# An attention block with a gated bilinear FFN: PSUM redistributed between score slots and free banks, x transposed on TensorE, a halved Q buffer and a longer ring

## The chip, the core and the metric

The kernel runs on one core of a Trainium2 chip. The metric is device microseconds for one execution. The core has five engines that matter here: PE (TensorE, matmuls), ACT (ScalarE, here the exponential), DVE (VectorE), POOL (GpSimd) and SP, which issues most DMAs. PE writes its results to PSUM, which this kernel divides into eight banks of 128 x 512 float32 values. Executions of one kernel spread here (the changed kernel: 801.4 to 813.0 us in four), so times below come with their runs, and the main argument rests on profiles, in which the same time can be followed item by item.

Ratios are computed as the mean time of one kernel's fast runs over the mean of the other's fast runs of the same rounds, so they are not quite the ratios of the medians quoted beside them.

## The reference, cut to what matters

```python
# x: [1, 2048, 512] bf16; 32 heads of 16; F = 1376
g = sigmoid((x * gate_w).sum(-1, keepdims=True))
q, k, v = split(x @ wqkv)                      # 32 heads
p = softmax(q @ k.T * 16 ** -0.5)              # 32 x 2048 x 2048 scores
a = (p @ v) @ wo
b = ((x @ w_gate) * (x @ w_up)) @ w_down
return g * a + (1 - g) * b
```

The 32 x 2048 x 2048 scores set the time. They are cut into 2048 **units** of 128 keys x 512 queries, one PSUM bank each. Four units (four heads of one parity) on the same 128 keys form an **entry**, and 16 entries form a **group**; there are 32 groups.

## The kernel before

An order model inside the kernel builds one static program for each engine. Each unit takes one of two routes. ACT reads two or three banks of scores at once and writes exp to a ring PT in SBUF. Or DVE clamps the scores to int16 (one bank at a time, buffer I2), then makes four integer copies of the whole entry (LL and I2 again), which read as bf16 approximate exp. PE then multiplies by V ("PV"), accumulating in psO. All other matmuls (K, Q, V, FFN, output projection) are **fill units**: they need a bank for a few matmuls and one eviction by DVE.

The eight banks are two score slots of three, one for PV and one free bank:

```python
psS = psum_tensor("psS", [128, 3072], F32)   # two slots of three banks
psO = psum_tensor("psO", [128, 512], F32)
psX = psum_tensor("psX", [128, 512], F32)    # the one free bank
```

The third bank of a slot is lent out. When a span of scores is planned, it has three units, or two if the third bank goes to a late fill unit or to a DVE score:

```python
tf, of = third_free(sl)
n, fu, dj = 3, None, None
if tf > max(now, r) + 0.02:
    n = 2
else:
    f = pick_fill(now + 0.3) if now < D_START or F_LATE else None
    if f is not None and f.due + F_LATE <= st["prog"] / 4 and un[0][0][0] < NG - 1:
        n, fu = 2, f                      # a late fill unit takes the third bank
    elif un[0][0][0] == NG - 1 and sl == 0:
        n = 2
    elif not (x_free() and ...) and backlog(now) < D_BACK:
        dj = d_can(now, {j for _, j in un[:2]}, False)
        if dj is not None:
            n = 2                         # a DVE score takes the third bank
```

x comes in transposed by 16 transposing DMAs; Q has two buffers and is asked for 14 entries before its block:

```python
QX = sb("QX", [128, 2, 2, NB, 512], BF16)    # chunk parity, head parity, block
PT = sb("PT", [128, RU, 512], BF16)          # RU = 18
...
o = ld("sp", xT[:, kt, ch * 512 : (ch + 1) * 512],
       x2[ch * 512 : (ch + 1) * 512, kt * 128 : (kt + 1) * 128], ..., transpose=True)
...
n0 = 128 * c + 32 * b - 14                   # Q for row chunk c, block b
fl.append((n0, mk_q(b, c, n0)))
```

In the last group the softmax denominators use one more bank (the third of the first slot), and the tail computes 1/denominator as exp(-ln) in four column slices, Ln then Exp for each slice.

The softmax here doesn't subtract the row's maximum and nothing guards it: scores larger than these inputs give would overflow.

## Time and profile before

857.75 us median of 3 runs (854.71 to 858.06). The profiled execution's span is 858.1 us. It was a further execution of 859.96 us, in the slow state (a lower granted clock, 0.928); it is some 2 us slower than the median, so about 2 us of the account below may be its state.

From the page of the kernel before: busy time by engine, then, in 40 slices of the span, the busy tenths of ACT and DVE and the granted TensorE clock in tenths.

```profile
PE 774.0 (90%) x6164; PEld 200.7 (23%) x6164; DVE 628.9 (73%) x1010; ACT 778.7 (91%) x759; POOL 36.1 (4%) x34
DVE  1326689988989973787998479897967599896401
ACT  1427999999999998899999989999999999999997
PEclk9857969999999999889999999999999999999856
```

ACT is 91% busy and is full from slice 5 on; the first four slices are thin, and there the granted clock falls to 0.5. (The trace's first clock event is at 28.0 us. Up to there the view shows full clock, but the matmuls stand 0.43 us apart, the pace of half clock, so the first digits are not a measurement.) The groups view names what ACT and DVE do. Columns: line, engine, operation, output and input, count, busy us, mean ns of one, idle time just before, and what ended that idle time.

```profile
L1259 ACT ACTIVATE PT<-psS 128x1024 bf16<-128x1024 f32 (+1 forms) x740 | 764.6, 1236 | 71.1 <-PE psS L748 51.7 <-PE psO L987 9.7 <-PE psS L864 7.6
L887 DVE TENSOR_SCALAR I<-psS 128x512 int16<-128x512 f32 x329 | 220.9, 685 | 35.7 <-PE psS L864 34.6
L887 DVE TENSOR_SCALAR I<-psX 128x512 int16<-128x512 f32 x55 | 37.7, 686 | 9.9 <-PE psX L864 9.5 <-PE psS L748 0.2
L918 DVE TENSOR_SCALAR LL<-I 128x2048 int16<-128x2048 int16 x288 | 194.6, 704 | 3.5 <-PE psO L987 2.0
L918 DVE TENSOR_SCALAR I<-I 128x2048 int16<-128x2048 int16 x96 | 70.1, 730 | 1.6
```

L1259 is the exponential: 740 spans, 764.6 us busy, 71.1 us idle before it. L887 is the DVE clamp: 329 scores taken from slot banks (psS) and 55 from the free bank (psX), 384 units in all, so ACT has 2048 - 384 = 1664. L918 makes the copies.

The timeline of ACT from 20 to 70 us (start, duration, operation, count, and in brackets the idle time before and its releaser):

```profile
20.21 4.35 ACT L1259 ACTIVATE PT<-psS 128x1536 bf16<-128x1536 f32 x3 [14.58 <-PE psS L748]
25.04 1.45 ACT L1259 ACTIVATE PT<-psS 128x1536 bf16<-128x1536 f32 x1 [0.48 <-PE psS L748]
30.42 5.48 ACT L1259 ACTIVATE PT<-psS 128x1536 bf16<-128x1536 f32 x4 [3.92 <-PE psS L748]
46.50 5.57 ACT L1259 ACTIVATE PT<-psS 128x1536 bf16<-128x1536 f32 x4 [10.61 <-PE psS L748]
64.28 5.58 ACT L1259 ACTIVATE PT<-psS 128x1536 bf16<-128x1536 f32 x4 [12.20 <-PE psS L748]
```

Between 20 and 70 us ACT sits idle for most of the time, waiting for score matmuls. Stretches of the span (columns: stretch, its length, then busy us and instruction count of PE, PEld, DVE, ACT and POOL, granted clock, DMA share, GB/s):

```profile
40.00:60.00 20.00, 15.04 (x52) 3.21 (x48) 5.61 (x9) 5.57 (x4) 0.00 (x0) 0.50 0.00 1
200.00:300.00 100.00, 96.41 (x834) 25.40 (x832) 92.30 (x150) 100.00 (x103) 2.61 (x2) 1.00 0.07 16
300.00:400.00 100.00, 92.46 (x727) 23.59 (x723) 72.37 (x116) 91.85 (x93) 2.77 (x2) 0.95 0.07 19
```

At 40 to 60 us ACT works 5.6 of 20 us at half the matmul clock. At 200 to 300 us ACT is full and DVE at 92%. At 300 to 400 us ACT loses 8 us and DVE 28.

The span splits along ACT: 20.2 us until the first exponential, 764.6 us of exponentials, 56.5 us of waits between them (71.1 less the 14.6 before the first), and 16.7 us from the last exponential to the end.

### The profile page before, as it was taken

The numbers are of one execution on the slowest core, as the hardware profiler recorded it, in microseconds if no ns is written. First come the engines' busy times: TensorE is split into PE (matmuls) and PEld (weight loads), VectorE is DVE, ScalarE is ACT, GpSimd is POOL, SyncE is SP. The second block draws the span as 40 slices with busy tenths as digits, with TensorE's granted clock in tenths as the row PEclk, the third lists the DMA queues.
The fourth block names the chain that finished last, engine by engine and source line by source line (L and its number), as shares of the span: only waits on it lengthen the run. The fifth ranks groups of instructions, "written<-read, shape, count | busy, mean of one in ns | idle before, by whom it ended". The sixth has DMA issues, their size and how long they took to land.

```text
span 858.1 us, 15166 instructions
## 1 busy us (share of the span) xinstructions
PE 774.0 (90%) x6164; PEld 200.7 (23%) x6164; DVE 628.9 (73%) x1010; ACT 778.7 (91%) x759; POOL 36.1 (4%) x34
## 2 busy tenths in 40 slices
PE   3777998899999999898999999998999999999895
PEld 0111312222222222222222222222222222222211
DVE  1326689988989973787998479897967599896401
ACT  1427999999999998899999989999999999999997
POOL 6000000000000000000000000000000000000000
PEclk9857969999999999889999999999999999999856
DMA  8700000000000000000000010000001100000000
GB/s 153 246 1 1 14 21 13 21 15 20 7 15 21 14 26 20 26 12 10 21 11 21 21 33 12 23 13 9 21 7 28 32 20 15 18 15 8 17 18 24
DMA packets 35657, 22.36 MB, mean 26 GB/s; under 512 B 23012, under 2 KB 30532, under 8 KB 35588
## 3 DMA queue, kind: packets, MB, share of 16 engines
q1 hardware_dynamic: 32420, 19.83, 8.8%
q10 hardware_dynamic: 3168, 1.57, 0.9%
q8 instruction: 48, 0.79, 0.4%
q14 instruction: 21, 0.17, 0.1%
HBM read 10.65 MB, written 2.35 MB: 15 GB/s over the span
## 4 chain that ended last, share of the span: by engine, by line
PE 38%; ACT 32%; DVE 16%; issue 7%; SPq 4%; DMA 3%; ACTq 0%; DVEq 0%
ACT PT L1259 30%; PE psS L748 12%; PE psO L987 10%; DVE I L887 5%; DVE LL L918 5%; PE psX L504 3%; PE psX L426 3%; SPq L410 2%; PE psX L555 2%; DVE I L918 2%; PE psS L555 2%; SPq L1037 1%; DVE VV L434 1%; DMA xT<-in_A_x_dram 1%; PE psX L342 1%
## 5 line engine op out<-in xcount | busy, mean ns | idle before, releaser
L1259 ACT ACTIVATE PT<-psS 128x1024 bf16<-128x1024 f32 (+1 forms) x740 | 764.6, 1236 | 71.1 <-PE psS L748 51.7
L748 PE MATMUL psS<-QX,KT 32*128 32x512 bf16 x1664 | 300.5, 406 | 38.1 <-ACT PT L1259 27.6
L887 DVE TENSOR_SCALAR I<-psS 128x512 int16<-128x512 f32 x329 | 220.9, 685 | 35.7 <-PE psS L864 34.6
L918 DVE TENSOR_SCALAR LL<-I 128x2048 int16<-128x2048 int16 x288 | 194.6, 704 | 3.5 <-PE psO L987 2.0
L987 PE MATMUL psO<-PT,VV 128*32 128x512 bf16 x1664 | 163.9, 407 | 6.9 <-DVE VV L434 6.4
L748 PEld LDWEIGHTS psS<-QX,KT 32*128 32x128 bf16 x1664 | 71.1, 91 | 324.3 <-ACT PT L1259 257.2
L864 PE MATMUL psS<-QX,KT 32*128 32x512 bf16 x329 | 129.0, 392 | 0.2
L987 PE MATMUL psO<-LL,VD 128*32 128x512 bf16 x768 | 72.8, 397 | 0.5 <-DVE LL L918 0.4
L918 DVE TENSOR_SCALAR I<-I 128x2048 int16<-128x2048 int16 x96 | 70.1, 730 | 1.6
L987 PEld LDWEIGHTS psO<-PT,VV 128*32 128x32 bf16 x1664 | 40.0, 96 | 79.5 <-issue 58.5
L1090 POOL TENSOR_TENSOR OT<-onum,rb 128x512 bf16<-128x512 f32 x16 | 22.6, 1415 | 788.8 <-DMA rb<-rscr 788.8
L504 PE MATMUL psX<-xT,wg 128*128 128x512 bf16 (+1 forms) x160 | 51.9, 400 | 1.1 <-DVE usb L518 0.9
L504 PE MATMUL psX<-xT,wu 128*128 128x512 bf16 (+1 forms) x148 | 50.0, 403 | 0.9 <-DVE hT L528 0.5
L887 DVE TENSOR_SCALAR I<-psX 128x512 int16<-128x512 f32 x55 | 37.7, 686 | 9.9 <-PE psX L864 9.5
L987 PE MATMUL psO<-LL,VV 128*32 128x512 bf16 x384 | 39.5, 402 | 4.7 <-DVE LL L918 2.6
L987 PE MATMUL psO<-I,VD 128*32 128x512 bf16 x384 | 39.0, 397 | 2.3 <-DVE I L918 2.2
L434 DVE CAST VV<-psX 128x512 bf16<-128x512 f32 x16 | 11.1, 693 | 31.6 <-PE psX L426 31.6
L426 PE MATMUL psX<-wv,xT 128*128 128x512 bf16 x64 | 28.1, 568 | 5.5 <-DVE VD L447 3.1
L528 DVE TENSOR_TENSOR hT<-psX,usb 128x512 bf16<-128x512 f32 (+1 forms) x40 | 27.3, 682 | 5.5 <-PE psX L504 5.5
L864 PEld LDWEIGHTS psS<-QX,KT 32*128 32x128 bf16 x329 | 30.0, 91 | 1.7 <-DMA QX<-Qst 0.8
L555 PE MATMUL psX<-wd,hT 128*128 128x512 bf16 (+1 forms) x99 | 29.4, 384 | 0.4 <-DVE bsb L566 0.2
L518 DVE CAST usb<-psX 128x512 bf16<-128x512 f32 (+1 forms) x37 | 25.2, 680 | 5.3 <-PE psX L504 5.3
(84 smaller groups left out, 360.9 us busy)
## 6 DMA issues: line engine op xcount, KB each, us to landing
rb<-rscr SPq DMA_DIRECT2D x16, 256.0 KB
onum<-oraw SPq DMA_DIRECT2D x124, 32.0 KB, 2.0
out_dram<-ost SPq DMA_DIRECT2D x16, 128.0 KB, 1.7
QX<-Qst SPq DMA_DIRECT2D x120, 16.0 KB, 1.8
wu<-in_B_w_up_dram SPq DMA_DIRECT2D x1, 1376.0 KB, 6.2
wg<-in_B_w_gate_dram SPq DMA_DIRECT2D x1, 1376.0 KB, 9.0
wd<-in_B_w_down_dram SPq DMA_DIRECT2D x1, 1280.0 KB, 12.2
wv<-in_A_wqkv_dram ACTq DMA_DIRECT2D x1, 512.0 KB, 6.3
```

The costliest lines, as they stand in the source:

```text
L426: return pe.matmul(bk, xT[:, kt, t * 128 : (t + 1) * 128], wv[:, kt, :], start=s0, stop=s1)
L504: return pe.matmul(bk[0:w, :], ws[:, kt, f * 128 : f * 128 + w], xT[:, kt, c * 512 : (c + 1) * 512], start=s0, stop=s1,)
L518: "dve", lambda v: v.tensor_copy(usb[0:w, n % 2, :], un.bank[0:w, :]), deps, **EV
L528: lambda v: v.tensor_tensor(hT[0:w, f, :], un.bank[0:w, :], usb[0:w, n % 2, :], ALU.mult),
L555: return pe.matmul(bk, hT[0:w, f, tt * 128 : (tt + 1) * 128], wd[0:w, f, :], start=s0, stop=s1)
L748: q = pe.matmul(bank_ap(sl, k_), KT[32 * j : 32 * j + 32, b, kt * 128 : (kt + 1) * 128], QX[32 * j : 32 * j + 32, c % 2, p, b, :], start=True,
L864: lambda pe: pe.matmul(bank, KT[32 * j : 32 * j + 32, b, kt * 128 : (kt + 1) * 128], QX[32 * j : 32 * j + 32, c % 2, p, b, :], start=True, ...
L887: lambda v: v.tensor_scalar(I2[:, nb, j, :], bank, _LO, _HI, ALU.max, ALU.min),
L918: lambda v: v.tensor_scalar(dstt, src, 0.5, _BASE + _OFF[k], ALU.mult, ALU.add),
L987: r = pe.matmul((psD if dn else psO)[32 * j : 32 * j + 32, :], ones[:, k_, :] if dn else vcol(m, kt, k_, j), lview(e, k, j) if isd else PT ...
L1090: lambda g: g.tensor_tensor(OT[:, c % 2, b, :], onum[:], rb[:], ALU.mult),
L1259: lambda a: a.activation(PT[:, cells[0] : cells[0] + n, :].rearrange("p a b -> p (a b)"), bank_ap(sl, 0, n), ACT.Exp, scale=_LN2 / _OCT,),
```

## The change

The intent is to give ACT fixed slots of three and two banks, and use the eighth bank as a second free bank that fill units and DVE scores share, so that a DVE score no longer shrinks a span. x is loaded plainly and transposed on PE, to start earlier. Q's buffer is halved, which pays for a ring of 24, and Q is asked for 24 entries ahead. DVE scores are also allowed in the last group. Not shown below: the K units of the start are due three entries earlier than before and the V units one. The core of the diff, with cuts:

```diff
-    RU = 18
+    RU = 24
-    D_LEFT = 6
+    D_LEFT = 4
+    D_LAST = 11
-    FFN_FROM, FFN_TO = 75.0, 490.0
+    FFN_FROM, FFN_TO = 60.0, 490.0
...
-        QX = sb("QX", [128, 2, 2, NB, 512], BF16)
+        QX = sb("QX", [128, 2, NB, 512], BF16)
...
+        xn = SC[:, 0:8192].bitcast(BF16).rearrange("p (t n) -> p t n", t=T)
...
-        psS = ... [128, 3072] ...
+        psS = ... [128, 2560] ...
-        psX = ... [128, 512] ...
+        psX = ... [128, 1024] ...
+        CAP = [3, 2]
+        XB = [psX[:, 0:512], psX[:, 512:1024]]
...
-        for ch in range(NCH):                 # 16 transposing DMAs
-            for kt in range(KD):
-                o = ld("sp", xT[...], x2[...], ..., transpose=True)
+        for t in range(T):                    # 16 plain loads
+            d_xn.append(ld("sp", xn[:, t, :], x2[t * 128 : (t + 1) * 128, :], ...))
...
+        def mk_x(t, due, eng="dve"):          # a fill unit: 4 transposes, 1 copy
+                return pe.transpose(o[:, kt * 128 : (kt + 1) * 128], xn[...], ident[:])
...
-            un = act_units(3)
+            un = act_units(CAP[sl])
...                                            # the choice of n, fu, dj is gone
-                n0 = 128 * c + 32 * b - 14
+                n0 = 128 * c + 32 * b - 24
...
+            xi = x_get(t)                      # a free bank, if there is one
+            if xi is not None:
+                f = pick_fill(t + 0.3)
+                if t > D_START and any(isinstance(x["u"], Unit) for x in xs):
+                    f = None                   # one fill unit at a time after the start
+                if f is not None:
+                    start_fill(f, XB[xi], xs[xi]["op"])
...
+                if s_ready > t + D_GAP:
+                    j = d_can(t, set())
+                    if j is not None:
+                        do_d(j, xi)            # a DVE score in a free bank
```

More of the change, by code (lines that the diff above doesn't have):

```diff
@@ L167, in _build @@
     NE = NG * T
-    RU = 18
+    RU = 24
     D_START = 60.0
-    D_LEFT = 6
+    D_LEFT = 4
+    D_LAST = 11
     D_GAP = 0.3
-    D_BACK = 1.3
-    F_LATE = 6
-    FFN_FROM, FFN_TO = 75.0, 490.0
+    FFN_FROM, FFN_TO = 60.0, 490.0
     VS = H * 17 + 16
@@ L203, in _build @@
         PT = sb("PT", [128, RU, 512], BF16)
-        I2 = sb("I2", [128, 2, 4, 512], I16)
-        LL = sb("LL", [128, 3, 4, 512], I16)
+        SC = sb("SC", [128, 10240], I16)
+        LL = SC[:, 0:6144].rearrange("p (k j n) -> p k j n", k=3, j=4)
+        I2 = SC[:, 6144:10240].rearrange("p (k j n) -> p k j n", k=2, j=4)
+        xn = SC[:, 0:8192].bitcast(BF16).rearrange("p (t n) -> p t n", t=T)
+        ident = sb("ident", [128, 128], BF16)
         OT = sb("OT", [128, 2, NB, 512], BF16)
@@ L222, in _build @@
         warm = sb("warm", [128, 1], F32)
-        psS = stack.enter_context(nc.psum_tensor("psS", [128, 3072], F32))
+        psS = stack.enter_context(nc.psum_tensor("psS", [128, 2560], F32))
         psO = stack.enter_context(nc.psum_tensor("psO", [128, 512], F32))
-        psX = stack.enter_context(nc.psum_tensor("psX", [128, 512], F32))
+        psX = stack.enter_context(nc.psum_tensor("psX", [128, 1024], F32))
+        CAP = [3, 2]
+        XB = [psX[:, 0:512], psX[:, 512:1024]]
         P = _Plan()
@@ L234, in _build @@
         wcol = lambda lo, hi: A_wqkv[:, lo:hi].rearrange("(kt p) n -> p kt n", p=128)
-        d_x = []
-        for ch in range(NCH):
-            for kt in range(KD):
-                o = ld(
-                    "sp",
-                    xT[:, kt, ch * 512 : (ch + 1) * 512],
-                    x2[ch * 512 : (ch + 1) * 512, kt * 128 : (kt + 1) * 128],
-                    f"dx{ch}",
-                    dur=1.46,
-                    lat=6.0,
-                    transpose=True,
-                )
-            d_x.append(o)
+        d_xn = []
+        for t in range(T):
+            d_xn.append(ld("sp", xn[:, t, :], x2[t * 128 : (t + 1) * 128, :], f"dx{t}", dur=0.3, lat=2.2 + 0.3 * (t > 3)))
+        ev_x = {}
+        xdep = lambda ch: [ev_x[t] for t in range(4 * ch, 4 * ch + 4)]
         d_wk, d_wq = [None] * NB, [None] * NB
@@ L273, in pool_set @@
             return o
+        i0 = pool_set(ident[:], 1.0, 0.2)
+        o_id = P.op(
+            "pool",
+            lambda g: g.affine_select(
+                ident[:], ident[:], [[-1, 128]], ALU.is_equal, 0.0, base=0, channel_multiplier=1
+            ),
+            [i0],
+            dur=0.4,
+        )
+        prev.append(o_id)
         vcols = lambda a: a[:, :, 0 : 17 * H].rearrange("p t (h c) -> p t h c", c=17)
@@ L359, in drain, with mm, make @@
                 dve_push(1, [last], make)
-            return Unit(due, chain(KD, mm), lambda: [d_wk[b], d_x[ch]], drain)
+            return Unit(due, chain(KD, mm), lambda: [d_wk[b]] + xdep(ch), drain)
+        last_x = []
+        def mk_x(t, due, eng="dve"):
+            def mm(pe, bk, kt, s0, s1):
+                o = bk.bitcast(BF16)
+                return pe.transpose(o[:, kt * 128 : (kt + 1) * 128], xn[:, t, kt * 128 : (kt + 1) * 128], ident[:])
+            def drain(un, last):
+                if t == T - 1:
+                    last_x.append(last)
+                dst_ = xT[:, :, t * 128 : (t + 1) * 128]
+                src_ = lambda: un.bank.bitcast(BF16)[:, 0:512].rearrange("p (k n) -> p k n", k=KD)
+                def make():
+                    if eng == "dve":
+                        ev_x[t] = un.free = P.op("dve", lambda v: v.tensor_copy(dst_, src_()), [last], dur=0.33, lat=0.1)
+                    else:
+                        ev_x[t] = un.free = P.op(
+                            "act", lambda a: a.activation(dst_, src_(), ACT.Copy), [last], dur=0.5, lat=0.1
+                        )
+                if eng == "dve":
+                    dve_push(0, [last], make)
+                else:
+                    make()
+            return Unit(due, chain(KD, mm), lambda: [d_xn[t], o_id], drain, 0.06)
         qn = [0]
@@ L382, in make @@
                                 lambda v: v.tensor_scalar(
-                                    QX[:, 0, p, 0, :], un.bank, mask[:, p : p + 1], _QSCALE, ALU.mult, ALU.mult
+                                    QX[:, p, 0, :], un.bank, mask[:, p : p + 1], _QSCALE, ALU.mult, ALU.mult
                                 ),
@@ L410, in make @@
                                 lambda e, r0=r0, p=p: e.dma_start(
-                                    QX[r0 : r0 + 16, c % 2, p, b, :], Qst[r0 : r0 + 16, s, :]
+                                    QX[r0 : r0 + 16, p, b, :], Qst[r0 : r0 + 16, s, :]
                                 ),
-                                [ev_q[b, c], q_use.get((b, c - 2))] + ([o_qz] if c < 2 else []),
+                                [ev_q[b, c], q_use.get((b, c - 1))] + ([o_qz] if c < 1 else []),
                                 f"dq{s}",
@@ L420, in drain @@
                 dve_push(1, deps, make)
-            return Unit(due, chain(KD, mm), lambda: [d_wq[b], d_x[c]], drain)
+            return Unit(due, chain(KD, mm), lambda: [d_wq[b]] + xdep(c), drain)
         def mk_v(t, due):
@@ L455, in drain @@
                         dve_push(1, [last, o_vd], make)
-            return Unit(due, chain(KD, mm), lambda: [d_wv, d_x[t // 4]], drain)
+            return Unit(due, chain(KD, mm), lambda: [d_wv, ev_x[t]], drain)
         ogate = {}
@@ L494, in drain @@
                 act_q.append(([last], amake))
-            return Unit(due, grp, lambda: [d_gw] + d_x, drain, 0.25)
+            return Unit(due, grp, lambda: [d_gw] + [ev_x[t] for t in range(T)], drain, 0.25)
         def mk_ug(c, f, which, due):
@@ L535, in deps @@
             def deps():
-                r = [d_wu if which == "u" else d_wg, d_x[c]]
+                r = [d_wu if which == "u" else d_wg] + xdep(c)
                 if which == "u":
@@ L630, in grp @@
             return c, qd // 2, qd % 2
-        left = [[kt for kt in range(T) if kt not in DK] + list(DK) for _ in range(NG)]
+        left = [[kt for kt in range(T) if kt not in DK] + list(DK) if g else list(range(T)) for g in range(NG)]
         pv_done = [0] * NG
@@ L668, in _build @@
         spans = []
-        third = [None, None]
         active = []
@@ L681, in bank_ap, with x_get @@
             return psS[:, 1536 * sl + 512 * k : 1536 * sl + 512 * (k + n)]
-        def third_free(sl):
-            h = third[sl]
-            if h is None:
-                return 0.0, None
-            if h[0] == "x":
-                o = h[1]["x"]
-                return (1e9, None) if o is None else (o.done + P.SEM, o)
-            o = h[1].free
-            return (1e9, None) if o is None else (o.done + P.SEM, o)
-        den_hold = {"on": False}
+        xs = [dict(op=None, u=None, res=False) for _ in range(2)]
+        def x_get(now):
+            for x in xs:
+                if x["u"] is not None and x["u"].free is not None:
+                    x["op"], x["u"] = x["u"].free, None
+            for k, x in enumerate(xs):
+                if not x["res"] and x["u"] is None and (x["op"] is None or x["op"].done + P.SEM <= now + 0.02):
+                    return k
+            return None
         def backlog(now):
@@ L723, in do_s @@
             sl = i % 2
-            tf, of = third_free(sl)
-            n, fu, dj = 3, None, None
-            if tf > max(now, r) + 0.02:
-                n = 2
-            else:
-                f = pick_fill(now + 0.3) if now < D_START or F_LATE else None
-                if f is not None and f.due + F_LATE <= st["prog"] / 4 and un[0][0][0] < NG - 1:
-                    n, fu = 2, f
-                elif un[0][0][0] == NG - 1 and sl == 0:
-                    n = 2
-                elif not (x_free() and dst["xfree"].done + P.SEM <= now + 0.2 and pick_fill(now + 1) is None) and backlog(now) < D_BACK:
-                    dj = d_can(now, {j for _, j in un[:2]}, False)
-                    if dj is not None:
-                        n = 2
-            un = un[:n]
             n = len(un)
-            deps = list(kd) + ([spans[i - 2]["x"]] if i >= 2 else [])
-            if n == 3 and of is not None:
-                deps.append(of)
+            deps = list(kd) + ([spans[i - 2]["x"]] if i >= 2 else [o_s3])
+            if un[0][0][0] == NG - 1:
+                xs[1]["res"] = True
             def fn(pe):
@@ L750, in fn @@
                         KT[32 * j : 32 * j + 32, b, kt * 128 : (kt + 1) * 128],
-                        QX[32 * j : 32 * j + 32, c % 2, p, b, :],
+                        QX[32 * j : 32 * j + 32, p, b, :],
                         start=True,
@@ L764, in do_s @@
             spans.append(sp)
-            if n == 3:
-                third[sl] = ("x", sp)
-            if fu is not None:
-                start_fill(fu, bank_ap(sl, 2), of)
-                third[sl] = ("f", fu)
-            if dj is not None:
-                third[sl] = ("f", do_d(dj, bank_ap(sl, 2), of, dj in {j for _, j in un}))
-                return {j for _, j in un} | {dj}
             return {j for _, j in un}
@@ L785, in start_fill @@
             active.append(u)
-        dst = dict(e=None, js=[], buf=0, last_p1=None, p1={}, pend=0, xfree=None)
+        dst = dict(e=None, js=[], buf=0, p1={})
         d_free = [None, None]
@@ L791, in _build, with d_can @@
         l_wait = [None] * 3
-        def x_free():
-            u = dst.get("xf")
-            if u is not None:
-                if u.free is None:
-                    return False
-                dst["xfree"], dst["xf"] = u.free, None
-            return not dst["pend"]
-        def d_can(now, js_busy, in_x=True):
-            if in_x:
-                if not x_free():
-                    return None
-                if dst["xfree"] is not None and dst["xfree"].done + P.SEM > now + 0.02:
-                    return None
-            if dst["e"] is None:
-                if den_hold["on"]:
-                    return None
-                if not d_claim(now):
-                    return None
+        def d_can(now, js_busy):
+            if dst["e"] is None and not d_claim(now):
+                return None
             for j in dst["js"]:
@@ L819, in d_claim @@
         def d_claim(now):
-            if now < D_START:
+            if now < D_START or not last_x:
                 return False
@@ L826, in d_claim @@
                 return False
-            g = max(st["gD"], st["gA"])
-            while g < NG and (not [k for k in DK if k in left[g]] or (g == st["gA"] and len(left[g]) < D_LEFT)):
+            g = max(st["gD"], st["gA"], 1)
+            while g < NG and (not [k for k in DK if k in left[g]] or (g == st["gA"] and len(left[g]) < (D_LAST if g == NG - 1 else D_LEFT))):
                 g += 1
-            if g >= NG - 1 or g > st["gA"] + 1:
+            if g >= NG or g > st["gA"] + 1:
                 return False
@@ L848, in _build, with do_d @@
             free = None
-        def do_d(j, bank=None, of=None, clash=False):
-            in_x = bank is None
+        def do_d(j, xi, clash=False):
             h = Hold()
-            if in_x:
-                bank, of = psX[:], dst["xfree"]
+            bank, of = XB[xi], xs[xi]["op"]
+            xs[xi]["u"] = h
             e = dst["e"]
@@ L866, in do_d @@
                     KT[32 * j : 32 * j + 32, b, kt * 128 : (kt + 1) * 128],
-                    QX[32 * j : 32 * j + 32, c % 2, p, b, :],
+                    QX[32 * j : 32 * j + 32, p, b, :],
                     start=True,
@@ L878, in do_d @@
             q_use[b, c] = o
-            if in_x:
-                dst["xfree"] = None
-                dst["pend"] = 1
-            d4 = [o, d_free[nb]]
+            d4 = [o, d_free[nb] or last_x[0]]
             def make():
@@ L891, in make @@
                 h.free = x
-                if in_x:
-                    dst["xfree"] = x
-                    dst["pend"] = 0
                 dst.setdefault("p1ops", {}).setdefault(e, []).append(x)
@@ L903, in do_d @@
                 dst["e"] = None
-            return h
         def cheap(e, nb):
@@ L918, in make @@
                         lambda v: v.tensor_scalar(dstt, src, 0.5, _BASE + _OFF[k], ALU.mult, ALU.add),
-                        pops + ([lf] if k < 3 else done[:3]),
+                        pops + ([lf or last_x[0]] if k < 3 else done[:3]),
                         dur=0.6,
@@ L962, in vcol @@
             return a[:, o : o + 32]
-        psD = bank_ap(0, 2)
+        psD = XB[1]
         def do_pv(it):
@@ L976, in do_pv @@
             deps = list(p_op[it]) + [ev_vd[kt] if k_ else ev_v[kt]]
-            if first and m:
+            if first:
                 deps.append(o_ev[m - 1])
@@ L980, in do_pv @@
             if tail and first:
-                deps += [o_ones, third_free(0)[1]]
+                deps += [o_ones, xs[1]["op"] if xs[1]["u"] is None else xs[1]["u"].free]
             def fn(pe):
@@ L1100, in _build @@
         fl = []
-        fl += [(4 * ch - 3, mk_k(0, ch, 4 * ch - 3)) for ch in range(1, NCH)]
-        fl += [(t - 2, mk_v(t, t - 2)) for t in range(T)]
+        for ch in range(1, NCH):
+            n0 = 4 * ch - 6
+            fl += [(n0 - 0.2, mk_x(t, n0 - 0.2)) for t in range(4 * ch, 4 * ch + 4)]
+            fl.append((n0, mk_k(0, ch, n0)))
+        fl += [(t - 3, mk_v(t, t - 3)) for t in range(T)]
         fl.append((20, mk_gate(20)))
@@ L1128, in _build @@
         fills += [u for _, u in fl]
-        pro = [mk_k(0, 0, 0), mk_q(0, 0, 0)]
+        pro = [mk_x(t, 0, "dve" if t % 2 else "act") for t in range(4)] + [mk_k(0, 0, 0), mk_q(0, 0, 0)]
         for n_, u in enumerate(pro):
-            u.bank = psX[:] if n_ else psO[:]
+            u.bank = [XB[0], XB[1], psO[:], psS[:, 2048:2560], XB[0], psO[:]][n_]
+            of = [pro[0].free, pro[2].free][n_ - 4] if n_ > 3 else None
             for q_, mmf in enumerate(u.mms):
-                o = P.op("pe", (lambda pe, f=mmf, u=u: f(pe, u.bank)), u.deps() if q_ == 0 else [], "pe_f", dur=MM * 2, lat=0.2, mode="f")
-            u.drain(u, o)
-        while dve_q:
-            dve_q.sort(key=lambda x: x[0])
-            dve_q.pop(0)[2]()
-        dst["xfree"] = pro[1].free
-        o_ev[-1] = pro[0].free
+                o = P.op(
+                    "pe",
+                    (lambda pe, f=mmf, u=u: f(pe, u.bank)),
+                    u.deps() + [of] if q_ == 0 else [],
+                    "pe_f",
+                    dur=u.cost * 2,
+                    lat=0.2,
+                    mode="f",
+                )
+            u.drain(u, o)
+            while dve_q:
+                dve_q.sort(key=lambda x: x[0])
+                dve_q.pop(0)[2]()
+        xs[0]["op"], xs[1]["op"] = pro[4].free, pro[1].free
+        o_ev[-1] = pro[5].free
+        o_s3 = pro[3].free
         n_units = 4 * NE
@@ L1150, in step_pe @@
                 busy = do_s(t)
-                j = d_can(P.t["pe"], busy) if pick_fill(P.t["pe"] + 0.5) is None else None
-                if j is not None:
-                    do_d(j, clash=j in busy)
+                xi = x_get(P.t["pe"])
+                if xi is not None and (
+                    pick_fill(P.t["pe"] + 0.5) is None or any(isinstance(x["u"], Unit) for x in xs)
+                ):
+                    j = d_can(P.t["pe"], busy)
+                    if j is not None:
+                        do_d(j, xi, j in busy)
                 return True
@@ L1176, in step_pe @@
                 return True
-            if s_ready > t + D_GAP and pick_fill(t + 0.5) is None:
-                j = d_can(t, set())
-                if j is not None:
-                    do_d(j)
-                    return True
+            xi = x_get(t)
[5 more added lines that the diff above has]
+                    start_fill(f, XB[xi], xs[xi]["op"])
+                    xs[xi]["u"] = f
+                    return True
+                if s_ready > t + D_GAP:
+                    j = d_can(t, set())
+                    if j is not None:
+                        do_d(j, xi)
+                        return True
             pick = None
@@ L1217, in step_pe @@
                 return True
-            if x_free() and dst["xfree"].done + P.SEM <= t + 0.02:
-                f = pick_fill(t + 0.3)
-                if f is not None:
-                    start_fill(f, psX[:], dst["xfree"])
-                    dst["xf"] = f
-                    return True
             return False
@@ L1317, in _build @@
         c = NCH - 1
-        banks = [psX[:], bank_ap(1, 2), bank_ap(1, 0), bank_ap(1, 1)]
-        xs = [sp["x"] for sp in spans]
+        banks = [XB[0], bank_ap(1, 0), bank_ap(0, 0), bank_ap(1, 1)]
+        ex = [sp["x"] for sp in spans]
+        x_get(1e9)
+        xfree0 = xs[0]["op"]
         o_first = []
@@ L1322, in _build @@
             deps = [d_wo] + [o_mult[c, b] for b in range(NB)]
-            deps += [dst["xfree"]] if tt == 0 else [xs[-1], xs[-2], xs[-3]]
-            if tt == 1:
-                deps.append(third_free(1)[1])
+            deps += [xfree0] if tt == 0 else [ex[-1], ex[-2], ex[-3]]
             def fn(pe, tt=tt):
```

## The prediction

> **What bounds the kernel now.** The page gives ACT 91% busy, PE 90%, DVE 73%, the chain of waits the exponential 30%. Work is 2048 score units (128x512): ACT exponentiates 1664, DVE does 384 by integer arithmetic (329 from the slots' third bank, 55 from the free bank). The groups view: ACT 764.6 us for 1664 units, 0.46 us each, in 556 two-bank and 184 three-bank spans. A DVE entry of four units costs DVE 4 x 0.685 + 4 x 0.71 = 5.6 us and relieves ACT of 1.84.
>
> Three losses, by stretches and timeline:
> - Start, 0 to 100 us: only 103 ACT and 12 DVE units; ACT waits 43 us for score matmuls. x arrives by transposing DMA at 13.0 us, the first exponential starts at 20.2 us. 16 V and 3 K units then go one at a time through the single free bank: a V step takes 3.2 us (matmuls 1.83, eviction 0.69, PV 0.62), at a granted clock of 0.50 from 43 to 64 us. This agrees with the Trainium skill, "TensorE: Matmul & The Clock Gate", Part 1 (low activity halves the clock): matmuls are paced 0.43 us there, 0.215 later.
> - Steady, 100 to 800 us: ACT 97% busy, DVE 72 to 92% (best 200 to 300 us, with 61 DVE units); 2.67 units/us. Q moves late: eight issues of 0.6 us plus 1.8 us landing lie on the chain, and ACT idles 2.9 us at 341 us.
> - End: the last group is ACT alone, then a 17 us tail after the last exponential at 841 us.
>
> **What the change does.** Plain loads of x, 64 small transposes on PE and 16 short copies (estimate 6 and 5 us) replace the transposing DMA; Q clearing is halved. First exponential about 14 us (estimate, -6). Two free banks let a V matmul overlap the previous eviction; with a ring of 24 instead of 18 the V phase becomes PE bound, about 2.3 us per step. I expect some 190 units by 100 us instead of 115: 27 us gained.
> Fixed 3/2 spans: about 655 spans instead of 740, but ACT cost per unit barely changes (last group of before, already alternating 3/2: 9.28 us per 20 units, 0.464). PE saves 85 score phases and pays with separate DVE score matmuls.
> DVE scores no longer shrink a span and seldom wait for a bank: DVE about 92% busy from 65 us on, 56 units per 100 us; with ACT at 215 that is 2.71 units/us (+1.6%, 12 us). Q is requested 10 entries earlier, so its wait disappears although its buffer is halved. DVE in the last group saves 5 us. DVE entries: 96 to about 104.
>
> **Sum.** 26 us equivalent start + 2048/2.71 = 756 + 5 (last group) + 17 tail = 804; I say 806 us, range 786 to 830. Chances: faster 0.93, same 0.06, slower 0.01.
>
> **What would show it.** Right: first exponential near 14 us; ACT wait for score matmuls before 100 us below 20 us; about 650 exponentials, half 1536 wide; DVE over 80% of the span; 410 to 425 DVE units; no Q landing with ACT idle; tail 17 us.
>
> **What would make it wrong.** PE becomes the limit: separate DVE score matmuls and mode changes, or half clock during the V phase; then ACT idles in steady state. Fill work confined to one bank slips and leaves FFN after the last exponential.

## The result, and the profile after

803.89 us median of 4 runs (801.4 to 813.0) against 857.9 (854.71 to 858.88): ratio 0.9396, 95% interval 0.9318 to 0.9473. The output is correct. The profiled execution has a span of 803.0 us.

The page of the kernel after, the lines that answer to those of before:

```profile
PE 745.8 (93%) x6252; PEld 207.5 (26%) x6252; DVE 630.7 (79%) x1024; ACT 771.4 (96%) x688; POOL 32.9 (4%) x36
DVE  3647889888997875898977778986969879998732
ACT  3899999999999999999999999998999999999997
PEclk9998799999999999999999999998999999999986
```

ACT is at 8 tenths in the second slice and full from the third on, and the clock stays up in the slice where it had been at 5. The groups view of the kernel after, exponential (now L1263), DVE clamp (L876) and copies (L903):

```profile
L1263 ACT ACTIVATE PT<-psS 128x1536 bf16<-128x1536 f32 (+1 forms) x667 | 756.2, 1332 | 22.7 <-PE psS L766 19.5 <-PE psX L856 2.7
L876 DVE TENSOR_SCALAR SC<-psX 128x512 int16<-128x512 f32 x384 | 259.2, 684 | 82.9 <-PE psX L856 80.4 <-PE psS L766 1.8
L903 DVE TENSOR_SCALAR SC<-SC 128x2048 int16<-128x2048 int16 x384 | 258.0, 695 | 3.3
```

DVE takes **exactly as many units as before: 384**. Nothing moved from ACT to DVE. The exponentials are 667 spans instead of 740 and 8.4 us shorter in sum; the idle time before them fell from 71.1 to 22.7 us. The timeline of ACT in the same stretch as above:

```profile
14.68 14.58 ACT L1263 ACTIVATE PT<-psS 128x1536 bf16<-128x1536 f32 x13 [7.37 <-PE psS L766]
31.67 7.38 ACT L1263 ACTIVATE PT<-psS 128x1024 bf16<-128x1024 f32 x7 [2.41 <-PE psS L766]
41.18 18.19 ACT L1263 ACTIVATE PT<-psS 128x1536 bf16<-128x1536 f32 x16 [2.13 <-PE psS L766]
59.17 2.54 ACT L1263 ACTIVATE PT<-psS 128x1536 bf16<-128x1536 f32 x2
63.15 7.22 ACT L1263 ACTIVATE PT<-psS 128x1536 bf16<-128x1536 f32 x6 [1.45 <-PE psX L856]
```

The first exponential comes at 14.7 us, and the gaps after it that these lines show are 1.5 to 2.4 us; before, three of the four were 4 to 12. The same stretches as above, kernel after:

```profile
40.00:60.00 20.00, 18.96 (x181) 6.25 (x179) 9.98 (x18) 18.82 (x18) 0.00 (x0) 0.96 0.05 12
200.00:300.00 100.00, 93.78 (x824) 26.36 (x822) 85.09 (x136) 99.12 (x89) 3.08 (x2) 1.00 0.07 19
300.00:400.00 100.00, 93.76 (x799) 25.89 (x791) 84.45 (x137) 99.12 (x89) 2.91 (x2) 1.00 0.07 16
```

ACT works 18.8 of 20 us at 40 to 60 us and 99.1 of 100 at 300 to 400 us. At 200 to 300 us, where it was full before as well, nothing was to be gained.

The account of the span, item by item from the two profiles:

| | before | after | difference |
|---|---|---|---|
| start to first exponential | 20.2 | 14.7 | -5.5 |
| exponentials, busy | 764.6 | 756.2 | -8.4 |
| ACT waits after the first, before 100 us | 32.5 | 7.8 | -24.7 |
| ACT waits after 100 us | 24.0 | 7.5 | -16.5 |
| last exponential to end | 16.7 | 16.8 | +0.1 |
| sum | 858.0 | 803.0 | -55.0 |

The waits before 100 us are the groups view's idle time of the exponentials in that stretch (47.1 and 15.2 us) less the wait before the first one (14.6 and 7.4); the waits after 100 us are the rest of 71.1 and 22.7. The gain is mostly idle time of ACT (46.7 of 55.0 us): 30.2 us of it (5.5 and 24.7) lie before 100 us. Of the 16.5 us after 100 us the waits view names the releasers: before, ACT waited 9.1 us there for the score matmuls of its spans, 7.7 behind PV and 6.4 behind DVE scores; after, 6.5, none and 0.8.

### The profile page after: what moved, and what is told of

It is laid out like the page before. It is cut to its first block, busy times and chain, and to the rows that moved or that the text cites. A ratio compares the mean times of both kernels' runs of the same rounds, so it can differ in the third digit from the quotient of the medians.

```text
span 803.0 us, 15190 instructions
## 1 busy us (share of the span) xinstructions
PE 745.8 (93%) x6252; PEld 207.5 (26%) x6252; DVE 630.7 (79%) x1024; ACT 771.4 (96%) x688; POOL 32.9 (4%) x36
## 4 chain that ended last, share of the span: by engine, by line
ACT 52%; PE 29%; issue 12%; DVE 5%; DMA 1%; SPq 1%; ACTq 0%; DVEq 0%
ACT PT L1263 50%; PE psO L972 9%; PE psS L766 9%; PE psX L538 2%; DVE SC L903 2%; PE psX L589 2%; PE psX L856 2%; PE psX L348 2%; DVE SC L876 2%; PE psX L460 1%; PE psX L401 1%; DMA SC<-in_A_x_dram 1%; ACT L1349 1%; ACT L1348 1%; SPq L444 1%
## 5 line engine op out<-in xcount | busy, mean ns | idle before, releaser
L1263 ACT ACTIVATE PT<-psS 128x1536 bf16<-128x1536 f32 (+1 forms) x667 | 756.2, 1332 | 22.7 <-PE psS L766 19.5
L876 DVE TENSOR_SCALAR SC<-psX 128x512 int16<-128x512 f32 x384 | 259.2, 684 | 82.9 <-PE psX L856 80.4
L766 PE MATMUL psS<-QX,KT 32*128 32x512 bf16 x1664 | 264.8, 392 | 32.1 <-ACT PT L1263 27.4
L903 DVE TENSOR_SCALAR SC<-SC 128x2048 int16<-128x2048 int16 x384 | 258.0, 695 | 3.3
L856 PE MATMUL psX<-QX,KT 32*128 32x512 bf16 x384 | 145.4, 388 | 2.0 <-DVE SC L876 0.8
L766 PEld LDWEIGHTS psS<-QX,KT 32*128 32x128 bf16 x1664 | 63.7, 91 | 261.2 <-ACT PT L1263 233.7
L972 PE MATMUL psO<-SC,VD 128*32 128x512 bf16 x1152 | 108.8, 393 | 3.9 <-DVE SC L903 3.6
L856 PEld LDWEIGHTS psX<-QX,KT 32*128 32x128 bf16 x384 | 34.1, 91 | 34.2 <-DVE SC L876 15.4
L972 PEld LDWEIGHTS psO<-SC,VD 128*32 128x32 bf16 x1152 | 27.6, 95 | 53.0 <-DVE SC L903 21.8
L972 PE MATMUL psO<-SC,VV 128*32 128x512 bf16 x384 | 39.2, 399 | 0.7 <-DVE oraw L1015 0.2
L538 PEld LDWEIGHTS psX<-xT,wu 128*128 128x128 bf16 (+1 forms) x176 | 13.9, 100 | 32.5 <-issue 23.1
```

Source lines behind the costliest of these rows:

```text
L538: return pe.matmul(bk[0:w, :], ws[:, kt, f * 128 : f * 128 + w], xT[:, kt, c * 512 : (c + 1) * 512], start=s0, stop=s1,)
L766: q = pe.matmul(bank_ap(sl, k_), KT[32 * j : 32 * j + 32, b, kt * 128 : (kt + 1) * 128], QX[32 * j : 32 * j + 32, p, b, :], start=True, st ...
L856: lambda pe: pe.matmul(bank, KT[32 * j : 32 * j + 32, b, kt * 128 : (kt + 1) * 128], QX[32 * j : 32 * j + 32, p, b, :], start=True, stop=True,
L876: lambda v: v.tensor_scalar(I2[:, nb, j, :], bank, _LO, _HI, ALU.max, ALU.min),
L903: lambda v: v.tensor_scalar(dstt, src, 0.5, _BASE + _OFF[k], ALU.mult, ALU.add),
L972: r = pe.matmul((psD if dn else psO)[32 * j : 32 * j + 32, :], ones[:, k_, :] if dn else vcol(m, kt, k_, j), lview(e, k, j) if isd else PT ...
```

## Experiments

The theory (A in the expectations): in the first 100 us the second free bank let the V and K units overlap their evictions; later Q no longer comes late; x's new path is worth its 5.5 us. The rivals: x's path carries the start (B), the ring carries it (C), Q is irrelevant (D), or span sizes explain the rest (E, F). Twelve runs were made, each compared with the kernel before on the same chip; two of them were the changed kernel itself, as a control.

One thing mixes into every comparison. Each edit makes the order model plan anew, and the number of DVE scores changes with it: 384 in the controls and a_best, 388 in a_bank80 and a_dmaxq36, 392 in a_dmax, a_ru18, a_q36 and b_q24, 396 in a_q14, 376 in a_cap22 and 216 in a_onebank. A score that DVE takes saves ACT about 0.45 us, so a difference of up to 5 us can come from this alone.

### a_ctl and a_ctl2: the control

> The changed kernel again, unedited, as the control on this chip for the other runs of this call. Expected 0.940 of the kernel before (801 to 806 us), with 384 DVE score units, ACT waiting under 25 us in all.

Median 810.98 us (805.05 to 811.28), ratio 0.9498 (0.9425 to 0.9571): above the expected 0.940, so the changed kernel varies. Its profile has 384 DVE scores, as expected, and 27.0 us of ACT waits instead of under 25.

> The changed kernel unedited, as the control of this call. 0.940 to 0.950 of the kernel before, some executions near 811 us where the matmul clock was granted low for a stretch.

Median 807.35 us (800.34 to 816.93), ratio 0.9393 (0.9335 to 0.945).

What goes with the spread can be seen. The 14 executions of the three sets (the result's four, a_ctl's four, a_ctl2's six) fall into two halves: seven of 800.3 to 805.1 us with a mean granted clock of 0.969 to 0.981, and seven of 810.6 to 816.9 us with 0.956 to 0.964. Stretches of 4 us, first of the kernel after, then of a_ctl, the same program:

```profile
552.00:556.00 4.00, 3.47 (x26) 0.75 (x26) 0.88 (x2) 3.65 (x4) 0.00 (x0) 0.66 0.14 33
556.00:560.00 4.00, 4.00 (x24) 1.00 (x20) 0.67 (x2) 2.48 (x2) 0.00 (x0) 0.50 0.08 10
560.00:564.00 4.00, 4.00 (x33) 1.09 (x36) 3.87 (x7) 3.54 (x3) 0.00 (x0) 0.99 0.20 66
564.00:568.00 4.00, 3.89 (x45) 1.05 (x37) 3.96 (x7) 4.00 (x5) 1.56 (x1) 1.00 0.00 0
```

```profile
552.00:556.00 4.00, 3.04 (x27) 0.67 (x23) 1.42 (x3) 3.65 (x4) 0.00 (x0) 0.67 0.09 21
556.00:560.00 4.00, 4.00 (x23) 0.83 (x24) 1.04 (x2) 2.75 (x3) 0.00 (x0) 0.50 0.10 20
560.00:564.00 4.00, 3.67 (x15) 0.88 (x14) 2.12 (x4) 2.55 (x3) 0.00 (x0) 0.50 0.20 61
564.00:568.00 4.00, 4.00 (x17) 0.57 (x16) 3.19 (x4) 2.38 (x3) 1.27 (x1) 0.50 0.03 7
```

Both drop to half clock at the same place in the program; one recovers after 6.8 us, the other after 20.5 (beyond the lines shown, near 574 us; a_ctl2's profile, of 811.26 us, does the same), and at half clock ACT works only about 2.5 of 4 us. So an episode costs a few us, by its length, and single executions of this kernel can't be compared more closely than about 10 us. What starts and ends an episode was not tested. In all 14 profiles each half-clock stretch that ended before the program did lasted a whole multiple of 3.41 us: two and six of them here, twelve (40.96 us, from 34.8 us on) in the start of the kernel before. In the Trainium skill's "TensorE: Matmul & The Clock Gate", Part 1, low activity halves the clock; the two traces don't settle whether that is what happened here. From 548 to 552 us PE was busy for 3.6 and 3.2 of 4 us and idle for at most 1 us at a time, and in the kernel after it had been no busier (3.3 of 4 us) from 544 to 548, at full clock.

### a_bank80: the second bank withheld in the start

```diff
             for k, x in enumerate(xs):
+                if k == 1 and now < 80.0:
+                    continue
```

> The changed kernel, but the second free bank is not handed out before 80 us of the order model; later everything as in the change. Theory A (in the first 100 us the V and K units were serialised by one bank, and the second bank is the largest part of the gain at the start): 14 to 20 us slower than the control, a V step near 3 us again, granted clock falling to about 0.5 to 0.7 between 40 and 65 us, the steady stretches unchanged. Rival B (the start gained because x comes earlier, not by transposing DMA): at most 5 us slower.

Median 827.83 us, ratio 0.9691 against the control's 0.9498: 16.9 us slower by medians, within theory A's 14 to 20. Three of a_ctl's four executions were of the low-clock half; against the ratios of the other two sets (0.9396 and 0.9393) it would be about 25 us. Two lines of the ACT timeline of a_bank80:

```profile
43.54 2.37 ACT L1265 ACTIVATE PT<-psS 128x1536 bf16<-128x1536 f32 x2 [10.16 <-PE psS L768]
...
65.70 2.37 ACT L1265 ACTIVATE PT<-psS 128x1024 bf16<-128x1024 f32 x2 [11.36 <-PE psS L768]
```

And its stretch from 40 to 60 us:

```profile
40.00:60.00 20.00, 16.23 (x59) 3.71 (x60) 6.19 (x11) 7.80 (x7) 0.00 (x0) 0.50 0.00 0
```

The gaps of 10 and 11 us are back, and so is the clock of 0.50. The last V eviction ends at 83.8 us; in the kernel before it ended at 83.0, in the kernel after at 51.3. By 100 us ACT has started 110 units and DVE 6; the kernel after 171 and 24, the kernel before 103 and 12. So without the second bank the V phase is as slow as before. ACT waits 27.1 us more than in a_ctl before 100 us; 6.3 us of waits are given back later, where this run has fewer of them.

Two things qualify this. The single bank of a_bank80 also has to pass x's transposes: where a new chunk's K and four transposes go between, its V evictions stand 12.0, 10.2 and 10.8 us apart; in the kernel before, with K alone between, 4.2, 6.9 and 6.9. So the loss belongs to a start with transposes; one bank beside the old transposing DMA was not run. And its plain V steps (those without the three extra evictions for DVE's copies of V) took 1.8 to 2.4 us at full clock but 3.3 to 3.6 at half clock, so part of the loss is the half clock that came with the single bank, and no run parts the two.

### a_dmax: x by transposing DMA again

The edit, cut to what matters:

```diff
+        for ch in range(NCH):                  # the 16 transposing DMAs of before
+            for kt in range(KD):
+                o = ld("sp", xT[...], x2[...], ..., transpose=True)
-            fl += [(n0 - 0.2, mk_x(t, n0 - 0.2)) for t in range(4 * ch, 4 * ch + 4)]
-        pro = [mk_x(t, ...) for t in range(4)] + [mk_k(0, 0, 0), mk_q(0, 0, 0)]
+        pro = [mk_k(0, 0, 0), mk_q(0, 0, 0)]
```

> The changed kernel with x brought by the old transposing DMA; two banks, fixed slots, ring of 24 and the halved Q buffer stay; the 64 transposes and 16 copies are gone. Theory A: 5 to 9 us slower than the control, since the first exponential moves from 14.7 to about 20 us and the rest of the start keeps its pace. Rival B: 20 us or more slower. If the transposes on the matmul engine cost what they save, no difference.

Median 804.18 us, ratio 0.9433 (0.937 to 0.9496), control 0.9498: not slower. Both A's 5 to 9 us and B's 20 fail; the third sentence of the expectation holds. The ACT timeline of a_dmax:

```profile
18.97 40.78 ACT L1273 ACTIVATE PT<-psS 128x1536 bf16<-128x1536 f32 x36 [13.27 <-PE psS L777]
59.45 2.65 ACT L1273 ACTIVATE PT<-psS 128x1536 bf16<-128x1536 f32 x2
63.32 7.04 ACT L1273 ACTIVATE PT<-psS 128x1536 bf16<-128x1536 f32 x6 [1.23 <-PE psS L777]
```

The first exponential is 4.3 us later than in the kernel after (18.97 against 14.68), but then ACT runs 40.8 us without a wait, where the kernel after waits 2.41 and 2.13 us for the units that K, V and the transposes of the next chunk delay. By 100 us ACT has started 173 units here and 171 there, and the V phase ends at 51.7 us against 51.3. So the early start is given back by then, in the waits that this run, without the 64 transposes and 16 copies, does not have.

### a_ru18: the ring at 18 cells

```diff
-    RU = 24
+    RU = 18
```

> The changed kernel with the ring of exponentials back at 18 cells. Theory A: within 3 us of the control, since the exponential engine never waits for ring space in steady state and only a little in the start. Rival C (the longer ring carries the start, letting the exponential run ahead of V): 6 us or more slower, all before 100 us.

Median 804.37 us, ratio 0.9421 (0.9338 to 0.9503), control 0.9498: no loss. By 100 us ACT has started 173 units, DVE 27. The longer ring does nothing that these runs can see, and rival C, which asked for 6 us before 100 us, falls. (This run's 8 more DVE scores save ACT some 3 us, which could hide a loss of that size. Its profiled execution was slow, so its later part is not compared.)

### a_q14 and a_q36: when Q is asked for

```diff
-                n0 = 128 * c + 32 * b - 24
+                n0 = 128 * c + 32 * b - 14     # a_q14;  - 36 in a_q36
```

> The changed kernel with Q for the later 512-row chunks asked for 14 entries ahead, as before, instead of 24; the Q buffer stays halved. Theory A (part of the steady gain is that Q no longer comes late): 3 to 10 us slower than the changed kernel (0.940 to 0.950 of the kernel before), with ACT waiting 1 us or more at several of the 12 block starts. Rival D (two free banks start the Q unit at once anyway): within 3 us.

Median 825.61 us, ratio 0.9607 (0.9529 to 0.9684). Theory A's direction holds, but its size was set too small: 15 and 18 us above the control's two medians (810.98 and 807.35) instead of 3 to 10. They were run at other times. From the timeline of a_q14 at the start of the second 512-row chunk, the eviction of Q, its eight DMA issues and the exponential that waited:

```profile
310.54 0.69 DVE L435 TENSOR_SCALAR Qst<-psX 128x512 bf16<-128x512 f32 x1 [0.61 <-PE psX L401]
311.26 4.94 SPq L444 DMA_DIRECT2D QX<-Qst  x8
317.49 0.11 PEld L766 LDWEIGHTS psS<-QX,KT 32*128 32x128 bf16 x3 [5.10 <-DMA QX<-Qst]
317.50 0.61 PE L766 MATMUL psS<-QX,KT 32*128 32x512 bf16 x3 [4.61 <-DMA QX<-Qst]
...
318.16 2.37 ACT L1263 ACTIVATE PT<-psS 128x1536 bf16<-128x1536 f32 x2 [7.79 <-PE psX L856]
```

DVE evicts Q at 310.5 us, eight issues take 4.9 us, the last landing 1.8 us, and ACT has waited 7.79 us. The other two chunk starts wait 5.4 and 6.3 us. Smaller waits follow each. The profiles add up to 21 us more ACT waiting than in a_ctl (48.0 against 27.0), less 5.2 us of exponentials, since DVE took 12 scores more. After 100 us ACT waits 31.8 us here, more than the 24.0 of the kernel before: by this profile the new banks without the earlier Q save no waiting in the steady part.

> The changed kernel with Q asked for 36 entries ahead instead of 24. Theory A (the fill queue, served by one bank at a time, delivers Q late; 24 is just in time, 14 was too late): no waits of 1 us or more at the three starts of a 512-row chunk, 1 to 6 us faster than the control. Rival: 24 was enough, within 1 us.

Median 801.84 us, ratio 0.9337 (0.93 to 0.9375); the control 0.9393 (0.9335 to 0.945). In its profile ACT waits no more than 0.4 us at any of the three chunk starts, so 24 was just in time (the kernel after waits 0.76 us for Q at 311 us). The medians differ by 5.5 us in the expected direction, but the intervals overlap, and the profile's exponentials are 4.5 us shorter in sum (752.6 against a_ctl2's 757.1), since DVE took 8 scores more, which would account for most of it: a gain from the earlier Q is not shown.

### b_q24: the earlier Q in the kernel before

```diff
-                n0 = 128 * c + 32 * b - 14
+                n0 = 128 * c + 32 * b - 24
```

> The kernel before with Q asked for 24 entries ahead and nothing else. Theory A: 4 to 8 us faster than the kernel before (ratio 0.990 to 0.995), its ACT wait of 2.9 us at 341 us gone, start and end unchanged. Rival D: no difference, ACT waits the same 21 us between 100 and 805 us.

Median 854.69 us against 856.85, ratio 0.9936 (0.9862 to 1.001). The wait at 341 us is gone, but the ACT waits in sum are not (71.3 us against 71.1): others of 6.4 us at 319 and 4.2 at 494 appeared, behind PE work. The ratio lies in theory A's 0.990 to 0.995, but not for A's reason: the profile's span is 4.5 us shorter, its exponentials are 4.8 us shorter (8 more DVE scores), and the waits are unchanged, as rival D has it. So in the old kernel the Q lead gave no waits back. It was the new kernel that needed it. The code gives a likely reason, which no run isolates: the old kernel could put a late fill unit into a slot's third bank at once; the new one runs one fill unit at a time, in order of due time, so Q queues behind the FFN's units.

### a_cap22: slots of two banks

```diff
-        CAP = [3, 2]
+        CAP = [2, 2]
```

> The changed kernel with two-bank slots only (one bank stays unused): 836 exponentials instead of 667. Theory E (larger spans pay: each exponential has a fixed cost of about 0.05 us and each span one more score phase of about 0.32 us on PE): 8 to 20 us slower than the changed kernel, 8 us of it in the busy time of the exponential, the rest in waits for PE. Rival F (span sizes don't matter, the banks do): within 4 us.

Median 852.55 us, of four executions of which two were slow; the fast ones give 0.9857 (0.9747 to 0.9967), class unclear. By ratios (0.9396 to 0.9498 for the changed kernel) it is some 30 to 40 us slower, more than theory E's upper limit of 20. The groups view of the profiled execution (839.7 us):

```profile
L1263 ACT ACTIVATE PT<-psS 128x1024 bf16<-128x1024 f32 x836 | 772.2, 1139 | 43.0 <-PE psS L766 25.4 <-PE psX L856 15.7 <-PE psO L972 1.4
```

836 spans take 16.0 us more than 667. The program holds 94 DVE entries instead of 96, so 8 units of the 16.0 us are ACT's at 0.45 us, 3.6 us; the other 12.4 us are 0.073 us for each of 169 more spans. The waits grew by 20.3 us, of which 7.1 are one wait for Q that ended at 328 us. Span size counts, but this run mixes it with a late Q, and the part of each in the waits stays open.

### a_onebank: the second bank withheld throughout

```diff
-        xs = [dict(op=None, u=None, res=False) for _ in range(2)]
+        xs = [dict(op=None, u=None, res=k == 1) for k in range(2)]
```

> The changed kernel with the second free bank never handed out (kept for the last group's denominators). The order of the program then holds 54 DVE entries instead of 96. Theory A (DVE scores and fill work need a bank each once the third bank of a slot is fixed to ACT): 168 more units on ACT at 0.45 us and the slow start again, 890 to 920 us, slower than the kernel before. Rival: only the start suffers, about 825 us.

998.54 and 1021.37 us, 79 and 101 us above the upper end of the expectation and far worse than the kernel before. The profile is of the slower. The 168 more units show (844.1 us of exponentials), but ACT also waits 151.8 us, in pieces of up to 15.8 us, and the clock is 0.815. Both sizes in the expectation fail. Once the third bank of the slots is fixed to ACT, one free bank is not enough for fill and DVE scores, in the whole span and not only in the start.

### a_dmaxq36 and a_best

The first a_dmax run had a wait of 6.8 us for Q at 308 us. With Q asked for 36 entries ahead the comparison of x's paths is cleaner:

> The transposing DMA for x again, now with Q asked for 36 entries ahead, so that the 6.8 us wait for Q that the first such run had at 308 us does not blur the comparison. Against a_q36: if the TensorE transposes are a gain, 3 us or more slower; if they cost in the start what the earlier x gives, within 2 us; if they are a loss, faster. I expect within 3 us either way, with the first exponential 4 us later and no ACT wait between 20 and 59 us.

Median 802.61 us, ratio 0.9356 (0.9307 to 0.9406), beside a_q36's 801.84 and 0.9337. The first exponential starts at 18.68 us (a_q36: 15.90) and ACT does not wait from 20 to 59 us. Within 3 us, as expected (with 4 fewer DVE scores, under 2 us): x's path is worth nothing in the total that these runs can show.

a_best combines plain loads for the first 512 rows, transposing DMA for the rest, Q 36 ahead, and one Ln for all columns in the tail (the tail's part of the edit):

```diff
-        for tt in range(4):
-            a1_ = P.op("act", lambda a, cs=cs: a.activation(lnd[:, cs], psD[:, cs], ACT.Ln), ...)
+        a1_ = P.op("act", lambda a: a.activation(lnd, psD, ACT.Ln), [lastpv] + free, dur=0.6)
+        for tt in range(4):
```

> A version meant to beat both: x for the first 512 rows by plain loads and TensorE transposes, the rest by the transposing DMA; Q asked for 36 entries ahead; in the tail one Ln over all 512 columns, then the four Exp, so two table loads of 1.28 us instead of eight. First exponential at 14 to 16 us; time from the last exponential to the end 9 to 11 us instead of 17; 8 to 14 us faster than the control (0.925 to 0.935 of the kernel before).

Median 805.8 us, ratio 0.939 (0.9341 to 0.944), control 0.9393: no gain. Its two parts worked in the profile. ACT runs from 15.9 us for 40.8 us without a wait, and the tail is 12.5 us instead of 16.8 (9 to 11 expected), with two table loads instead of eight:

```profile
790.72 1.28 ACT L1358 ACT_TABLE_LOAD   x1
792.01 0.60 ACT L1358 ACTIVATE oraw<-psX 128x512 f32<-128x512 f32 x1
792.63 1.28 ACT L1361 ACT_TABLE_LOAD   x1
793.92 0.91 ACT L1361 ACTIVATE rb<-oraw 128x128 f32<-128x128 f32 x4
```

But this program order has a longer half-clock stretch (the page shows 7, 7 and 8 tenths in slices 5 to 7) and another at its end; ACT waits 14.8 us after 100 us instead of the 7.5 of the kernel after. So some 4 us of tail and 3 us of start were lost again, probably to the clock: all its six executions have a lower mean clock (0.945 to 0.965) than a_q36's (0.971 to 0.976). This was not tested further. No version that beats the changed kernel clearly was found; a_q36 is the nearest.

## Why the prediction was right

The time (806 us predicted, 803.89 measured), its range and its class held. Point by point:

- **The bound and the start: right.** 190 units by 100 us were predicted, 195 measured (171 + 24). The V phase ran at 2.4 us a step (16 V from 12.2 to 51.3 us) against 2.3 predicted and about 4.1 before (18.2 to 83.0 us, stalls for K included). First exponential 14.7 us against "about 14", ACT waits for score matmuls before 100 us 13.1 us against "below 20". a_bank80 shows that the second bank is needed for it, in a start with the transposes.
- **"First exponential about 14 us (estimate, -6)": right in place, wrong as a gain.** a_dmax and a_dmaxq36 give the 4 us back and end at the same time, because ACT then waits for units that the DMA version has in time.
- **"with a ring of 24 instead of 18": this part of the step fell.** a_ru18 loses nothing.
- **"DVE about 92% busy from 65 us on ... DVE entries: 96 to about 104": wrong.** DVE is 79% busy over the span (just under the "over 80%"), and the entries are 96 again. DVE waited 80.4 us in the new kernel for its own score matmuls, by the groups view. Why the order model issues no more of them, since a DVE score may only start when a bank is free, no due fill claims it and the next span is not close, was not tested and stays open.
- **Steady rate 2.71 units/us: right, for another reason, and in part by luck.** From 100 us to the last exponential 1853 units took 686.2 us, 2.70 units/us (before: 1933 in 741.4 us, 2.61). It was to come from DVE at 56 units per 100 us, and DVE made 52.5 (360 in 686 us). It came mostly from ACT, at 217.6 units per 100 us against the 215 predicted and 210.5 before: its waits after 100 us fell by 16.5 us and its spans by 8.4 us, where I had put ACT's cost per unit at "barely changes" (measured 0.4595 and 0.4544 us). So DVE fell 3.5 units per 100 us short and ACT came out 2.6 over: two misses that nearly cancel. No run isolates which part of the change took the steady waits away; a_q14 shows that the earlier Q is needed for it, a_cap22 that span size counts (at its 0.073 us a span, the 73 fewer spans are worth 5.3 us, an estimate).
- **Q: direction right, size too small.** "its wait disappears although its buffer is halved" holds nearly (0.76 us at 311 us). But the lead is not a small refinement: without it the new kernel loses 15 to 18 us (a_q14), and in the old one it takes no waits away (b_q24).
- **Last group 5 us, tail 17 us: right.** The last group took 24.5 us from the start of its predecessor's eviction to the last exponential instead of 28.9, with two DVE entries in it; the tail 16.8 us.
- **PE at full clock:** PE did not become the limit, but half-clock episodes remain, and go with the spread of 801 to 813 us.

## What to carry to other kernels

When several kinds of work queue for PSUM, count banks by what each wait costs: here withholding the second free bank in the start put 27 us of waiting into the first 100 us (17 us in the total), since the short units then went one at a time. Once urgent units lose their private way to a bank, their lead must grow with the queue before them, and the lead is to be tested in the new kernel, not the old one. An earlier start counts only if the work that makes it early does not delay what follows: compare the units started by a later time, not the time of the first.

## What the Trainium skill lacked or had wrong

- "TensorE: Matmul & The Clock Gate", Part 1, says that the ramp penalty is under 1% of a typical kernel span. That is said of the warm-up at a kernel's start and is not contradicted here, but it is no measure of half clock as a whole: that stood for 14% of the span before (mean clock 0.928, so 2 x 0.072, from the first clock event on) and 6% after (0.970), and single episodes of 7 and 20 us begin in mid-kernel, with PE idle for no more than about 1 us at a time just before (near 553 us in the two runs shown). The page's account of idle windows does not say why such an episode lasts 7 us in one execution and 20 us in another of the same program.
- "ScalarE: Activation LUTs", What ACT_TABLE_LOAD costs, gives 1283 ns for the load and 1380 ns more of drain at each switch. The loads here take 1.28 us, but the next activation starts 1.30 us after the load's start (786.25 and 787.55 us in the tail of the kernel after), and a whole Ln and Exp round takes 3.22 us (two loads, 0.28 and 0.31 us): the drain does not show.
- The same section gives 186 ns plus 0.833 ns per column for an ACTIVATE with immediate operands, and an overlap of about 93 ns. Single exponentials here (a scale that is a number, no bias given) take 1.45 us for 1536 columns and 1.02 for 1024, so about 0.17 us fixed; in the full stretch from 100 to 200 us of the kernel after the pitch is 0.833 ns per column plus about 0.054 us (45 of 1536 and 44 of 1024 columns in 99.9 us), so the overlap is nearer 0.12 us.
- "DMA: Bandwidth & Descriptors", DMA Transpose (X-bar), lists TensorE as an alternative path and says it is useful when data is already on chip. No page says what it costs the rest of a kernel: here the first exponential came 3 to 4 us earlier with the transposes on TensorE, and the total did not change (802.61 us by DMA against 801.84).
